# Clustered attention in float32: probability tiles of 512 columns, codes by DMA, value sums off VectorE, a table load moved, due times replaced

## The chip, the core and the metric

The kernel runs on one core of one Trainium2 chip. The core has TensorE (PE in the profile), VectorE (DVE), ScalarE (ACT) and GpSimd (POOL); SyncE (SP) only issues DMAs here. Each engine takes its own instructions strictly in the order of the program. The metric is the device time of one execution in microseconds: 778.55 us before the change, the median of 3 runs that lie between 778.21 and 780.17.

## The reference

Sixteen heads (2 batches of 8), each of 768 tokens and width 64. Queries and keys attend to each other only when their nearest centroid is the same one; two matrix products with relu6 follow.

```
q_assign = argmax(q_n @ c_n^T)           # 16 centroids a head, normalized
k_assign = argmax(k_n @ c_n^T)
scores   = where(q_assign == k_assign, q @ k^T / 8, -1e9)
attn     = exp(scores - max); attn /= sum(attn) + 1e-9
x = attn @ v                             # -> 1536 x 512
h = (x @ w1) * (x @ w2); x = h @ w3 @ w_out
y = x @ w_in; y = y * clip(y + 3, 0, 6) / 6; out = y @ w_out2
```

All weights arrive as float64 and are converted on the chip with integer operations. Products are made in three float32r passes: every operand is split into a high part (ScalarE rounds it to float32r) and a low part (the rest, a subtraction).

## The kernel before

**The order is planned.** Every operation is entered with an engine (or several to choose from), a cost, what it needs, buffers ("rings") that it takes and drops, and a due time. The method `order` walks through them: among the operations that could start first on each engine it picks the one with the smallest due time. The table `SHIFT` adds a correction to single due times. What comes out is one list, and each engine runs its part of it in that order. So a change of costs, of an operation's engine or of `SHIFT` moves instructions on all engines.

**Attention, one head after the other.** `prep_ops(h)` loads q, k and v, splits them, transposes them on PE (`stack_T`, tile `pt`), copies them out (`stack_C`) and duplicates a half by DMA (`stack_D`). `assign_mm` computes the centroid products (tile `pa`), and nine small steps (`oh_step`, `oh0` to `oh8`) make the one-hot codes of the assignments; the last is a DVE transpose into the tile `cd`. `codes_C` then copies four pieces of 16 x 384 from `cd` into the operands `kA` and `qA`, which makes the mask a part of the score product. It runs on ACT or DVE (entry `Co`), whichever the plan finds free first.

`attn_ops(h)` has six chunks of 128 queries. For each, PE computes scores (`S1` of 512 columns and `S` of 256, two matmuls each, tile `pst`), DVE takes the maximum over 768 columns (`mx`, tile `den`), ACT the exponential with its row sum (`ex`, tile `p`; six buffers). The probabilities are then transposed on PE: `p_T` puts three 128 x 128 blocks into a PSUM bank (tile `ptr`, one of three buffers of ring `s`), 12 such tiles a head; `p_hi` rounds the 384 columns to `ph` on ACT, `p_lo` writes the rest to `pl` on DVE, and `av` multiplies by the values, with `vs` holding the high and low part of v in its two halves. So the product `av` has two halves of 64 rows that must be added. ACT copies one half to tile `O` (`o_copy`, `oc`). For the first two pairs of heads ACT copies the other half too (`o_copy2`, `oa`) and POOL adds them (`o_sum`, `os`); for the other six pairs DVE adds the halves (`o_add`), reading one of them from PSUM. `oap(h)` decides which. The row sums get 1e-9 added and are inverted on DVE (`den_recip`, `dr`), go through PE and DRAM (`rd`, `rdb`), and POOL multiplies them in (`pair_mul`, `pm`).

**Beside attention** PE has work that fills gaps: first the product of w3 and w_out (tiles `pt` for its transposes, `psw`), whose operands come from the conversions `c0` to `c5` (ACT, POOL, and three DVE steps), then, from head 9 on, the products of the first batch (`ab_mm`, tile `psab`). At the start `idle` matmuls keep PE busy. After attention come `psx`, a second `psab`, `psh` and `po`, the two feed-forward stages.

**SP** holds all DMA issues in one queue, also in the plan's order; an issue that waits for its buffer holds all behind it.

At the very start ACT loads a function table for its copies, one for the square root of the centroids' norms (`cen_2`) and one for the exponential (`warm_exp`).

The places by line: `warm_exp` 286, `cen_2` 309, `codes_C` 415, `p_T` 549, `p_hi` 555, `p_lo` 561, `av` 565, `oap` 585, `o_sum` 594, `o_add` 597, `den_recip` 603. The copies and subtractions themselves are recorded at their helpers' lines: 205 and 214 on POOL, 208 on DVE, 211 on ACT.

Of the kernel before, what the change touches and what calls it, by code (L numbers as in the profile page):

```python
# [160 lines left out]
def cluster_attention_moe_kernel(  # L161
# [387 lines left out]
    def p_T(h, hf, s, i):  # L549
        pt = ptr[i] = ps_s.tile([128, 512], F32, tag="s", name="ptr")  # L550
        for c in range(3):
            nc.tensor.transpose(pt[:, blk(c)], pps[h, 3 * hf + c][:, blk(2 * s + i)], id_f)  # L552
# [1041 lines left out]
```

## Time and profile before

| | us |
|---|---|
| median of 3 runs | 778.55 |
| the profiled execution | 778.79 |
| its span, first to last instruction | 777.0 |
| PE busy | 754.0 (97%) |
| DVE busy | 662.7 (85%) |
| ACT busy | 542.0 (70%) |
| POOL busy | 266.3 (34%) |

The granted TensorE clock is 0.998 of full over the span, so the clock is not a matter here. A matmul's row lasts until its modelled end and overlaps the next, so "busy" says less of PE than the interval from one start to the next does. The first instruction of the stage behind attention (`psx`) starts at 395.31 us; up to there the span is called the attention stage below.

### The profile page before, as it was taken

How to read it: one execution, taken by the hardware profiler on the slowest of the kernel's cores; microseconds unless marked ns; L12 is line 12 of the kernel's file. 1: busy time of each engine (PE TensorE's matmuls, PEld its weight loads, DVE VectorE, ACT ScalarE, POOL GpSimd, SP SyncE). 2: the span in 40 equal slices, each digit the busy share in tenths (PEclk: the TensorE clock that was granted, in tenths of full speed). 3: DMA queues.
4: the chain of work that ended last, by engine and by line, in shares of the span. 5: the costliest groups of instructions: out<-in, count | busy, mean ns of one | idle time of the engine just before them, and what ended most of it. 6: DMA issues, size and time to landing. Idle time of an engine off the chain costs nothing.

```text
span 777.0 us, 12420 instructions
## 1 busy us (share of the span) xinstructions
PE 754.0 (97%) x4266; PEld 682.0 (88%) x4266; DVE 662.7 (85%) x1184; ACT 542.0 (70%) x1070; POOL 266.3 (34%) x295
## 2 busy tenths in 40 slices
PE   6899999999999999999999999999999999999998
PEld 5678787888888899999899999999989889898986
DVE  6989999999999989899998899979999877767742
ACT  6779898887887787777763665757666667555544
POOL 4835656454563564443233111621222211010100
PEclk9999999999999999999999999999999999999999
DMA  7453343323343543334234543374544424212102
GB/s 227 125 173 107 106 133 105 108 87 116 116 116 89 160 140 112 112 113 135 91 136 136 164 148 123 106 247 149 174 152 123 139 91 150 82 55 67 41 14 81
DMA packets 57038, 94.20 MB, mean 121 GB/s; under 512 B 5168, under 2 KB 33936, under 8 KB 56976
## 3 DMA queue, kind: packets, MB, share of 16 engines
q1 hardware_dynamic: 56976, 93.43, 38.3%
q8 instruction: 33, 0.54, 0.3%
q14 instruction: 29, 0.24, 0.1%
HBM read 71.34 MB, written 15.78 MB: 112 GB/s over the span
## 4 chain that ended last, share of the span: by engine, by line
PE 57%; DVE 10%; ACT 5%; POOL 2%; issue 2%; DMA 1%; SPq 0%; DVEq 0%; ACTq 0%
PE po L1486 14%; PE psh L1442 13%; PE psab L1131 8%; PE psab L880 6%; PE psx L994 4%; PE pst L527 4%; PE av L572 3%; PE ptr L552 3%; POOL cvt L744 2%; DMA m_gb<-set 1%; DVE pl L208 1%; ACT p L544 1%; DVE den L536 1%; DVE cvs L753 1%; DVE m_whl L208 1%
## 5 line engine op out<-in xcount | busy, mean ns | idle before, releaser
L744 POOL TENSOR_SCALAR cvt<-cvt 128x512 f32<-128x512 f32 x72 | 73.5, 1023 | 172.5 <-ACT cvt L211 147.0
L211 ACT ACTIVATE ph<-ptr 128x384 fp32r<-128x384 f32 x192 | 90.7, 487 | 37.5 <-PE ptr L552 36.8
L208 DVE TENSOR_TENSOR pl<-ptr,ph 128x384 fp32r<-128x384 f32 x192 | 102.9, 549 | 11.6 <-ACT ph L211 9.9
L544 ACT ACTIVATE p<-pst,den 128x768 f32<-128x768 f32 x96 | 86.5, 901 | 11.7 <-DVE den L536 11.3
L536 DVE TENSOR_REDUCE den<-pst 128x1 f32<-128x768 f32 x96 | 90.8, 946 | 4.5 <-PE pst L527 3.6
L552 PE MATMUL ptr<-id_f,p 128*128 128x128 f32 x576 | 88.1, 274 | 2.0 <-DVE rdr L614 0.5
L880 PE MATMUL psab<-xT,abhl 128*128 128x384 f32 x384 | 86.6, 348 | 0.1
L552 PEld LDWEIGHTS ptr<-id_f,p 128*128 128x128 f32 x576 | 68.9, 140 | 11.8 <-DVE pl L208 2.6
L527 PE MATMUL pst<-kB,qB 128*128 128x512 f32 x192 | 71.1, 374 | 3.5 <-ACT p L544 2.8
L572 PE MATMUL av<-ph,vs 128*128 128x384 f32 x192 | 69.4, 362 | 0.1
L880 PEld LDWEIGHTS psab<-xT,abhl 128*128 128x128 f32 x384 | 64.5, 189 | 2.1 <-DVE g L890 0.7
L572 PE MATMUL av<-pl,vs 128*128 128x384 f32 x192 | 65.0, 339 | 0.5 <-DVE pl L208 0.4
L527 PE MATMUL pst<-kA,qA 128*128 128x512 f32 x192 | 64.2, 339 | 0.0
L753 DVE SCALAR_TENSOR_TENSOR cvs<-raw,cvs 128x512 int32<-128x512 int32 x72 | 54.6, 761 | 0.4
L211 ACT ACTIVATE cvt<-raw 128x512 f32<-128x512 f32 x72 | 47.9, 669 | 8.3 <-DMA raw<-in_moe_w_dram 4.2
L211 ACT ACTIVATE m_sn<-psh 128x384 f32<-128x384 f32 x64 | 31.0, 485 | 32.4 <-PE psh L1442 32.0
L804 PE MATMUL psw<-woh,wT 128*128 128x512 f32 x128 | 51.9, 416 | 0.7 <-ACT W L211 0.4
L1464 ACT ACTIVATE tt<-m_sn,three 128x384 f32<-128x384 f32 x48 | 29.5, 616 | 32.8 <-DVE m_sn L1452 25.2
L757 DVE SCALAR_TENSOR_TENSOR cvs<-cvt,cvs 128x512 int32<-128x512 int32 x72 | 50.2, 702 | 0.2
L527 PEld LDWEIGHTS pst<-kB,qB 128*128 128x128 f32 x192 | 36.1, 188 | 12.9 <-ACT p L544 9.8
L1486 PE MATMUL po<-m_hl,m_gv 128*128 128x512 f32 x171 | 46.2, 394 | 0.0
L749 DVE TENSOR_SCALAR cvs<-cvt 128x512 int32<-128x512 int32 x72 | 33.9, 478 | 7.4 <-POOL cvt L744 5.1
(206 smaller groups left out, 1934.6 us busy)
## 6 DMA issues: line engine op xcount, KB each, us to landing
raw<-in_moe_w_dram SPq DMA_DIRECT2D x32, 512.0 KB, 3.6
m_gb<-set SPq DMA_DIRECT2D x64, 256.0 KB, 3.4
raw<-in_moe_w_out_dram SPq DMA_DIRECT2D x24, 512.0 KB, 3.3
raw<-in_moe_w_in_dram SPq DMA_DIRECT2D x16, 512.0 KB, 4.2
set<-cvs SPq DMA_DIRECT2D x32, 256.0 KB, 4.2
abp<-cvs SPq DMA_DIRECT2D x16, 256.0 KB, 2.0
b_gv<-abp SPq DMA_DIRECT2D x16, 256.0 KB, 3.0
qn<-in_q_dram SPq DMA_DIRECT2D x16, 192.0 KB, 4.9
```

The lines of the kernel that those rows point to most:

```text
L208: nc.vector.tensor_tensor(out=out, in0=a, in1=b, op=ALU.subtract)
L211: nc.scalar.activation(out=out, in_=in_, func=AF.Copy, **kw)
L527: x = mm(out=psr[:, t, ks_], lhsT=TT["q" + nm, h][:, i, cs_], rhs=flat(TT["k" + nm, h])[:, ks_], start=st, stop=sp)
L536: done["mx", n] = [other_banks(nc.vector.tensor_reduce(out=dens[h][:, 0, c:c + 1], in_=psS[h, c], axis=AX.X, op=ALU.max, negate=True), ("S ...
L544: done["ex", n] = [other_banks(nc.scalar.activation(out=flat(p), in_=psS.pop((h, c)), func=AF.Exp, bias=d[:, 0, c:c + 1], accum_out=d[:, 1 ...
L552: nc.tensor.transpose(pt[:, blk(c)], pps[h, 3 * hf + c][:, blk(2 * s + i)], id_f)
L572: mm(out=t[:, 0:HF], lhsT=vs_t[h][:, 2 * s + i, :], rhs=x_[:, i, :], start=(s == 0 and i == 0 and n == 0), stop=(s == 2 and i == 1 and n = ...
L744: (nc.gpsimd.tensor_scalar if e == "pool" else ts)(out=tf, in0=tf, scalar1=H_MAX, scalar2=-H_MAX, op0=ALU.min, op1=ALU.max)
L753: stt(out=s, in0=raws.pop(key)[:, :, 0], scalar=29, in1=s, op0=ALU.logical_shift_right, op1=ALU.bitwise_or)
L880: mm(out=ps[:, 0:HF], lhsT=s[:, w, a, blk(kk)], rhs=xT0[0][:, x_, kk, hf * HF:hf * HF + HF], start=(kk == 0 and n == 0), stop=(kk == KD - ...
L1442: mm(out=ps[:, 0:HF], lhsT=left(p, l, a, kk), rhs=x[:, x_, kk, :], start=(st and kk == 0 and m == 0), stop=(kk == 1 and m == 2), skip_grou ...
L1486: mm(out=outs[b, c], lhsT=g[:, a, blk(c % 3)], rhs=w[:, w_, :], start=(first and a == 0 and w_ == 0), stop=(last and a == 1))
```

## The change

Five edits and a new table:

1. The transposed probabilities are cut anew: the 36 blocks of a head are taken in the order in which `av` reads them and put four to a PSUM bank, so a head has nine tiles of 512 columns and not twelve of 384. `ph` and `pl` are one tile each, of three 512-column places used in turn. The fifth tile holds two blocks of the first half of the queries and two of the second.
2. From head 1 on the four code pieces go by DMA from SP's queue (due a little earlier: 2.3 units ahead of the head where it was 1.8); head 0 keeps the copies.
3. `oap` holds for seven of the eight pairs: ACT copies both value halves and POOL adds them; the last pair keeps DVE's addition.
4. The addition of 1e-9 becomes an ACT operation of its own (`dd`), and DVE only inverts.
5. A square root of a constant, due before all else on ACT, loads the root's table first.
6. `SHIFT` is another table.

```
-    "warm": 1.7, ("Tq", 0, 1): 1.6, ("Dq", 0): 1.6, ("Tk", 0, 0): 10.3, ("oh1", 0): -4.4, ("ex", 0, 1): -0.1,
+    "cen2": 10.2, ("idle", 4): 0.1, ("idle", 5): -0.1, ("cT", 0): 1.9, ("lk", 0): 0.5, ("CkB", 0, 0): -0.1,
...
-        "p": NP, "ph": 2, "pl": 2, "den": 2, ...
+        "p": NP, "ph": 3, "den": 2, ...
...
+    op("root", "act", 0.2, lambda: warm(AF.Sqrt), due=-60)
+    op("warm", "act", 1.4, lambda: warm(AF.Exp), ["cen2"], due=-13.85)
...
     def codes_C(e, h, nm, hf):
-        copy_on(e, t[0:NCL, hf, :], codes[h][r0:r0 + NCL, :])
+        if h:
+            nc.sync.dma_start(out=t[0:NCL, hf, :].bitcast(F32), in_=codes[h][r0:r0 + NCL, :])
+        else:
+            copy_on(e, t[0:NCL, hf, :], codes[h][r0:r0 + NCL, :])
...
+            dd = b - (2.3 if h else 1.8) + 0.5 * hf
...
+                    op(("C" + nm, h, hf), "dma", 0.2, lambda nm=nm, hf=hf: codes_C(None, h, nm, hf), nd, due=due, lat=2.0, **kw)
...
+    def p_blocks(n):
+        return [(f // 18, f % 18 // 3, f % 3) for f in range(4 * n, 4 * n + 4)]
+    def p_cols(n):
+        return slice(512 * (n % 3), 512 * (n % 3) + 512)
+    def p_T(h, n):
+        pt = phl[h, n] = ps_s.tile([128, 512], F32, tag="s", name="ptr")
+        for j, (hf, kb, c) in enumerate(p_blocks(n)):
+            nc.tensor.transpose(pt[:, blk(j)], pps[h, 3 * hf + c][:, blk(kb)], id_f)
+    def p_hi(h, n):
+        copy_act(PHL[0][:, p_cols(n)], phl[h, n])
+    def p_lo(h, n):
+        sub_dve(PHL[1][:, p_cols(n)], phl.pop((h, n)), PHL[0][:, p_cols(n)])
...
     def oap(h):
-        return h // 2 < 2
+        return h // 2 < 7
...
+    def den_add(h):
+        nc.scalar.activation(out=d[:, 2, :], in_=d[:, 1, :], func=AF.Copy, bias=1e-9)
     def den_recip(h):
-        nc.vector.tensor_scalar(out=d[:, 2, :], in0=d[:, 1, :], scalar1=1e-9, scalar2=None, op0=ALU.add)
         nc.vector.reciprocal(out=d[:, 2, :], in_=d[:, 2, :])
...
+        for n in range(9):
+            u = b + LT + 2 * n / 3
+            op(("pT", h, n), "pe", 0.436, ..., due=u, take=("s",), drop=("p",) * 3 if n in (4, 8) else ())
+            op(("ph", h, n), "act", 0.48, ..., due=u + 0.1, take=("ph",), ...)
+            op(("pl", h, n), "dve", 0.6, ..., due=u + 0.2, drop=("s",))
```

What the change does to the order shows at three places. First ACT from its first instruction on, before (`qA` and `kA` are cleared rows, `cst` is the centroids' norm, `qs` and `ks` the split q and k of head 0, `warm` the dummy exponential):

```order
L211 ACT_TABLE_LOAD
L211 ACTIVATE qA<-three 64x768
L211 ACTIVATE kA<-three 64x768
L310 ACT_TABLE_LOAD
L310 ACTIVATE cst<-cst 128x1
L211 ACTIVATE qs<-qn 128x6x64
L288 ACT_TABLE_LOAD
L288 ACTIVATE warm<-three 128x1
L211 ACTIVATE ks<-kn 128x6x64
```

and now:

```order
L303 ACT_TABLE_LOAD
L303 ACTIVATE warm<-three 128x1
L225 ACTIVATE qA<-three 64x768
L225 ACTIVATE kA<-three 64x768
L225 ACTIVATE qs<-qn 128x6x64
L326 ACTIVATE cst<-cst 128x1
L303 ACT_TABLE_LOAD
L303 ACTIVATE warm<-three 128x1
L225 ACTIVATE ks<-kn 128x6x64
```

Of three table loads two are left, and the one ahead of the norm is gone; the split of q now stands ahead of the norm.

Second, the codes of head 8. Before, they stand on ACT between probability tiles (`ph`) and an exponential (`p,den`):

```order
L211 ACTIVATE ph<-ptr 128x384
L211 ACTIVATE kA<-cd 16x384
L211 ACTIVATE qA<-cd 16x384
L211 ACTIVATE ph<-ptr 128x384
L211 ACTIVATE kA<-cd 16x384
L544 ACTIVATE p,den<-pst,den 128x768
L211 ACTIVATE qA<-cd 16x384
L211 ACTIVATE ph<-ptr 128x384
```

Now they are four issues in SP's queue, behind the load of a weight (`raw`), the broadcast of a row sum (`rdb`) and the store of a converted weight (`abp`), and ahead of the load of v:

```order
L755 DMA raw<-in_moe_w_dram 128x4x256
L650 DMA rdb<-rd_116 64x768
L899 DMA abp_85<-cvs 128x512
L434 DMA kA<-cd 16x384
L434 DMA qA<-cd 16x384
L434 DMA kA<-cd 16x384
L434 DMA qA<-cd 16x384
L383 DMA vn<-in_v_dram 128x384
```

All four have left ACT. On SP they can be held by what stands ahead of them.

Third, DVE around the same code transpose (`cd`), before (`cvs` are conversions of a weight, `den` the maxima and row sums):

```order
L453 STREAM_TRANSPOSE cd<-ohs 128x384
L601 TENSOR_TENSOR T<-av,O 64x384
L536 TENSOR_REDUCE den<-pst 128x1
L208 TENSOR_TENSOR pl<-ptr,ph 128x384 x2
L753 SCALAR_TENSOR_TENSOR cvs<-raw,cvs 128x512
L813 TENSOR_TENSOR W_493<-W_493,psw 128x512
L536 TENSOR_REDUCE den<-pst 128x1
L208 TENSOR_TENSOR pl<-ptr,ph 128x384 x2
L757 SCALAR_TENSOR_TENSOR cvs<-cvt,cvs 128x512
L605 TENSOR_SCALAR den<-den 128x6
L606 RECIPROCAL den<-den 128x6
```

and now:

```order
L472 STREAM_TRANSPOSE cd<-ohs 128x384
L222 TENSOR_TENSOR pl<-ptr,ph 128x512
L779 TENSOR_SCALAR cvs<-cvt 128x512
L558 TENSOR_REDUCE den<-pst 128x1
L222 TENSOR_TENSOR pl<-ptr,ph 128x512
L787 SCALAR_TENSOR_TENSOR cvs<-cvt,cvs 128x512
L783 SCALAR_TENSOR_TENSOR cvs<-raw,cvs 128x512
L558 TENSOR_REDUCE den<-pst 128x1
L222 TENSOR_TENSOR pl<-ptr,ph 128x512
L843 TENSOR_TENSOR W_496<-W_496,psw 128x512
L787 SCALAR_TENSOR_TENSOR cvs<-cvt,cvs 128x512
```

Between two maxima there were two subtractions of 384 columns; now there are one or two of 512. The addition of value halves (`T<-av,O`) and the small addition ahead of the reciprocal are gone.

## Rows read from the trace of the kernel before

**Rows 1.** Stretches: length, busy us (instructions) of PE, PEld, DVE, ACT, POOL; clock, DMA
```profile
0.00:22.00 22.00, 15.96 (x66) 12.67 (x67) 15.64 (x37) 14.07 (x24) 11.62 (x37) 0.92 0.76 245
22.00:75.00 53.00, 49.16 (x287) 40.42 (x286) 48.45 (x88) 43.21 (x92) 29.16 (x38) 1.00 0.44 129
75.00:275.00 200.00, 193.26 (x1207) 168.28 (x1205) 186.73 (x349) 167.66 (x362) 105.58 (x123) 1.00 0.38 113
275.00:375.00 100.00, 99.76 (x640) 94.41 (x640) 91.50 (x169) 75.89 (x166) 43.36 (x51) 1.00 0.38 121
375.00:395.30 20.30, 19.50 (x112) 17.22 (x110) 18.46 (x30) 14.30 (x25) 5.43 (x4) 1.00 0.48 154
395.30:640.00 244.70, 243.16 (x1305) 230.11 (x1306) 219.44 (x376) 151.47 (x268) 59.72 (x37) 1.00 0.44 141
```

**Rows 2.** Timeline of PE within head 8: start us, us, instruction
```profile
205.82 0.39 PE L804 MATMUL psw<-woh,wT 128*128 128x512 f32 x1
206.05 0.40 PE L804 MATMUL psw<-wol,wT 128*128 128x512 f32 x1
...
206.52 0.28 PE L527 MATMUL pst<-kB,qB 128*128 128x256 f32 x1
206.63 0.29 PE L527 MATMUL pst<-kA,qA 128*128 128x256 f32 x1
206.76 0.82 PE L552 MATMUL ptr<-id_f,p 128*128 128x128 f32 x6
207.33 0.42 PE L572 MATMUL av<-ph,vs 128*128 128x384 f32 x1
207.59 0.34 PE L572 MATMUL av<-pl,vs 128*128 128x384 f32 x1
```

**Rows 3.** The chain in order of time: start us, us, what
```profile
395.31 32.35 PE psx L994 x185
```

**Rows 4.** Groups by shape: busy us, mean ns of one, idle us before and releaser
```profile
L208 DVE TENSOR_TENSOR pl<-ptr,ph 128x384 fp32r<-128x384 f32 x192 | 102.9, 549 | 11.6 <-ACT ph L211 9.9
L211 ACT ACTIVATE ph<-ptr 128x384 fp32r<-128x384 f32 x192 | 90.7, 487 | 37.5 <-PE ptr L552 36.8
L208 DVE TENSOR_TENSOR wT<-pt,wT 128x512 fp32r<-128x512 f32 x16 | 10.8, 675 | 0.8 <-ACT wT L211 0.7
L211 ACT ACTIVATE wT<-pt 128x512 fp32r<-128x512 f32 x16 | 9.5, 596 | 5.2 <-PE pt L776 5.2
L211 ACT ACTIVATE kA<-cd 16x384 fp32r<-16x384 f32 x29 | 15.2, 523 | 3.1 <-DVE cd L453 2.5
L601 DVE TENSOR_TENSOR T<-av,O 64x384 f32<-64x384 f32 x24 | 13.2, 550 | 1.9 <-ACT O L211 1.4
L211 ACT ACTIVATE T<-av 64x384 f32<-64x384 f32 x8 | 3.9, 484 | 0.1
L595 POOL TENSOR_TENSOR T<-T,O 128x768 f32<-128x768 f32 x2 | 3.7, 1843 | 1.9 <-ACT T L211 1.9
L605 DVE TENSOR_SCALAR den<-den 128x6 f32<-128x6 f32 x16 | 7.7, 483 | 2.2 <-ACT p L544 2.2
```

**Rows 5.** Timeline of ACT at the start: start us, us, instruction
```profile
3.62 1.28 ACT L310 ACT_TABLE_LOAD   x1
4.91 0.20 ACT L310 ACTIVATE cst<-cst 128x1 f32<-128x1 f32 x1
```

**Rows 6.** SP's copies within SBUF (line 411): issue ns min/median/max; time to landing
```profile
L411 SPq DMA_DIRECT2D kA<-kB x16: 461/467/539, 11.5 to 336.8; - x16
...
DMA to landing us min/median/max: 2.5/2.6/4.2
```

**Rows 7.** Timeline: one conversion step of DVE alone, and one beside a subtraction of POOL
```profile
23.62 1.27 POOL L205 TENSOR_TENSOR wol<-cvs,woh 128x512 fp32r<-128x512 f32 x1
...
23.80 1.38 DVE L749 TENSOR_SCALAR cvs<-cvt 128x512 int32<-128x512 int32 x1
...
50.97 0.37 DVE L749 TENSOR_SCALAR cvs<-cvt 128x512 int32<-128x512 int32 x1
```

More of the change, by code (lines that the diff above doesn't have):

```diff
@@ L284, in cluster_attention_moe_kernel, with warm @@
     op("id", "dve", 0.14, lambda: nc.vector.tensor_copy(id_r, id_f), due=-40)
-    def warm_exp():
-        W_["warm"] = at.tile([128, 1], F32, tag="warm", name="warm")
-        nc.scalar.activation(out=W_["warm"], in_=three, func=AF.Exp)
+    def warm(func):
+        if "warm" not in W_:
+            W_["warm"] = at.tile([128, 1], F32, tag="warm", name="warm")
+        nc.scalar.activation(out=W_["warm"], in_=three, func=func)
     def zero_rows(t):
         copy_act(t[0:64], three[0:64].unsqueeze(2).to_broadcast([64, 2, HF]), scale=0.0)
-    op("warm", "act", 1.4, warm_exp, ["cen2"], due=-13.85)
+    op("root", "act", 0.2, lambda: warm(AF.Sqrt), due=-60)
+    op("warm", "act", 1.4, lambda: warm(AF.Exp), ["cen2"], due=-13.85)
     for i, t in enumerate((qA_[1], kA_[1])):
@@ L487, in prep_ops @@
         for hf in range(2):
-            dd = b - 1.8 + 0.5 * hf
-            fop("Co", ("Ck", h, hf), {"a": 0.375, "d": 0.47}, lambda e, hf=hf: codes_C(e, h, "k", hf),
-                (("oh8", h), ("Dk", h)), due=dd + 0.05)
-            fop("Co", ("Cq", h, hf), {"a": 0.375, "d": 0.47}, lambda e, hf=hf: codes_C(e, h, "q", hf),
-                (("oh8", h), ("Dq", h)), due=dd + 0.06, after=[("Ck", h, 0), ("Ck", h, 1), ("Cq", h, 0)] if hf else (),
-                drop=("cd",) if hf else ())
+            dd = b - (2.3 if h else 1.8) + 0.5 * hf
+            for nm in "kq":
+                last = nm == "q" and hf
+                kw = dict(after=[("Ck", h, 0), ("Ck", h, 1), ("Cq", h, 0)] if last else (), drop=("cd",) if last else ())
+                nd, due = (("oh8", h), ("D" + nm, h)), dd + (0.06 if nm == "q" else 0.05)
+                if h:
+                    op(("C" + nm, h, hf), "dma", 0.2, lambda nm=nm, hf=hf: codes_C(None, h, nm, hf), nd, due=due, lat=2.0, **kw)
+                else:
+                    fop("Co", ("C" + nm, h, hf), {"a": 0.375, "d": 0.47}, lambda e, nm=nm, hf=hf: codes_C(e, h, nm, hf), nd, due=due, **kw)
         op(("pa", h), "pe", 0.7, lambda: assign_mm(h), [("CqB", h, 0), ("CqB", h, 1), ("CkB", h, 0), ("CkB", h, 1),
@@ L547, in sexp @@
         pps[h, c] = flat(p)
[L549 to L552, printed above, removed]
-        phl[h, hf, s, i, "t"] = pt
-    def p_hi(h, hf, s, i):
-        if i == 0:
-            phl[h, hf, s] = (at.tile([128, 2, HF], F32R, tag="ph", name="ph", bufs=2),
-                             at.tile([128, 2, HF], F32R, tag="pl", name="pl", bufs=2))
-        copy_act(phl[h, hf, s][0][:, i], phl[h, hf, s, i, "t"][:, 0:HF])
-    def p_lo(h, hf, s, i):
-        ph, pl = phl[h, hf, s]
-        sub_dve(pl[:, i], phl.pop((h, hf, s, i, "t"))[:, 0:HF], ph[:, i])
+    PHL = []
+    def p_blocks(n):
[7 more added lines that the diff above has]
+    def p_hi(h, n):
+        if not PHL:
+            PHL.extend(at.tile([128, 1536], F32R, tag=t, name=t) for t in ("ph", "pl"))
+        copy_act(PHL[0][:, p_cols(n)], phl[h, n])
+    def p_lo(h, n):
+        sub_dve(PHL[1][:, p_cols(n)], phl.pop((h, n)), PHL[0][:, p_cols(n)])
     def av(h, hf, s):
@@ L568, in av @@
         t = avs[h, hf]
-        ph, pl = phl.pop((h, hf, s))
         for i in range(2):
-            for n, x_ in enumerate((ph, pl)):
-                mm(out=t[:, 0:HF], lhsT=vs_t[h][:, 2 * s + i, :], rhs=x_[:, i, :],
+            c0 = HF * ((2 * s + i + 2 * hf) % 4)
+            for n, x_ in enumerate(PHL):
+                mm(out=t[:, 0:HF], lhsT=vs_t[h][:, 2 * s + i, :], rhs=x_[:, c0:c0 + HF],
                    start=(s == 0 and i == 0 and n == 0), stop=(s == 2 and i == 1 and n == 1))
@@ L657, in attn_ops @@
                 drop=("r",))
+        for n in range(9):
+            u = b + LT + 2 * n / 3
+            op(("pT", h, n), "pe", 0.436, lambda n=n: p_T(h, n), sorted({("ex", h, 3 * x[0] + x[2]) for x in p_blocks(n)}),
+               due=u, take=("s",), drop=("p",) * 3 if n in (4, 8) else ())
+            op(("ph", h, n), "act", 0.48, lambda n=n: p_hi(h, n), (("pT", h, n),), due=u + 0.1, take=("ph",),
+               after=[("ph",) + divmod(9 * h + n - 1, 9)] * (h + n > 0))
+            op(("pl", h, n), "dve", 0.6, lambda n=n: p_lo(h, n), (("ph", h, n),), due=u + 0.2, drop=("s",))
         for hf in range(2):
@@ L660, in attn_ops @@
                 u = b + 3 * hf + s + LT
[L661 to L669 removed]
+                m = 3 * hf + s
                 op(("av", h, hf, s), "pe", 0.65, lambda hf=hf, s=s: av(h, hf, s),
[L671 removed]
+                   [("pl", h, n) for n in {(3 * m) // 2, (3 * m + 2) // 2}] + [("vlo", h)] + [("av", h, hf, s - 1)] * (s > 0),
                        due=u + LA,
[L673 removed]
+                   take=("a",) if s == 0 else (), drop=("ph",) * (1 + m % 2) + (("vs",) if hf and s == 2 else ()))
             if oap(h):
@@ L686, in attn_ops @@
         e = b + NC
-        op(("dr", h), "dve", 0.35, lambda: den_recip(h), [("ex", h, c) for c in range(NC)], due=e + 1)
+        op(("dd", h), "act", 0.2, lambda: den_add(h), [("ex", h, c) for c in range(NC)], due=e + 0.9)
+        op(("dr", h), "dve", 0.2, lambda: den_recip(h), (("dd", h),), due=e + 1)
         op(("dT", h), "pe", 0.11, lambda: den_T(h), (("dr", h),), due=e + 1.2, take=("s",), drop=("den",),
```

14 lines of the change are left out of this document (2 added, 12 removed), and 52 rows, old and new, of the table SHIFT.

## The prediction

> **What bounds the kernel now.** I read the stretches first [rows 1]. PE is the busiest engine in every one, and behind 395.3 us there is nothing to win on it: 243.2 of 244.7 us busy. The reader should see the pair PE and DVE next: from 75 to 275 us PE has 193.3 of 200 us and DVE 186.7 (93%), while from 275 to 375 PE has 99.8 of 100 with DVE at 91.5. Since a busy PE row runs on to its modelled end, I took what PE's work is worth from the starts of neighbours in the timeline [rows 2]: a 512-column matmul 0.23 us (205.82 to 206.05), one of 256 columns 0.115 (206.52 to 206.63), one of 384 columns 0.175 (185 `psx` in 32.35 us [rows 3]), and six transposes with one 384-column matmul 0.83 (206.76 to 207.59), so 0.109 a transpose.
>
> The attention stage ends at 395.31 us, where `psx` starts [rows 3]. By the code's loops it holds 192 score pairs of both widths (192 x 0.345 = 66.2), 848 transposes (576 of probabilities, 192 of q and k, 64 of w3, 16 of row sums: 92.4), 832 matmuls of 384 columns (384 values, 64 centroids, 384 `psab`: 145.6) and 232 of 512 (192 `psw`, 40 idle ones: 53.4). That is 357.6 us, so 37.7 us are lost to waits. They spread, at the mean of 0.156 us an instruction over the counts of the stretches [rows 1], as about 11.7 us before 22 us, 8.3 up to 75, 12.0 up to 275, 0.3 up to 375 and 2.9 up to 395. The prize is the middle, some 20 us, where DVE feeds PE: a maximum for every chunk, a low part for every tile, and three conversion steps for the weights of the filling work. Behind 275 us PE fills its gaps with `psab`, whose operands come sooner, and loses next to nothing.
>
> **The change part by part.** PE: nothing is removed. The 36 transposes a head stay 36, and a group of transposes shows no price of its own in [rows 2], so nine groups for twelve are worth 0.
>
> DVE in the attention stage [rows 4]. Low parts: 192 x 0.549 = 105.4 become 144 of 512 columns, which is the shape of w3's low part at 0.675, 97.2: -8.2. Value sums: 20 of 24 go at 0.550: -11.0. The addition of 1e-9: 16 x 0.483: -7.7. Of the 64 code copies eight stand on DVE, one is left, priced as on ACT at 0.523: -3.7. The new plan gives DVE four more copies of transposed q and k (384 columns, as the low parts 0.549): +2.2. Sum -28.4 us, 1.8 a head.
>
> ACT: high parts 192 x 0.487 = 93.5 become 144 x 0.596 = 85.8: -7.7. Code copies 56 to 3 at 0.523: -27.7. Value halves +20 x 0.484 = +9.7 [rows 4]. The addition is not in the trace on ACT; between a one-column operation at 0.20 [rows 5] and the 384 columns of 0.487 [rows 4] I take 0.20, which has nearly its size: +3.2 (to 7.8). The four copies to DVE: -1.9. Sum about -24 us.
>
> POOL: five more sums at 1.84 [rows 4], +9.2 on an engine that is busy 53% of the middle.
>
> The table: a load of 1.28 us stands right ahead of the norm on ACT [rows 5] and goes; the split of q, 384 columns or some 0.49 us, now stands there in its place. Everything to the first score hangs on this chain: -0.8, bounds -1.3 and 0 (0 if k's arrival decides).
>
> The codes: on ACT the three pieces that the first scores need take 3 x 0.523 = 1.6 us at least. By DMA three issues of 0.467 and a landing of 2.6 make 4.0 us, up to 5.6 with the slowest landing of 4.2 [rows 6], so 2.4 to 4.0 later. What hides it is the plan: in DVE's order the transpose that ends the codes stands two or more maxima ahead of its head's first one for 12 of 15 heads. From 22 to 395 us there are 16 heads, 23.3 us each and 3.9 a chunk, so that is over 7 us. Heads 1, 2 and 10 have one maximum, 3.9 us: 0.1 to 1.7 each may show. Below nothing there is nothing, since the score cannot start sooner than before by this. I take +1.0 for all, bounds 0 and +5. In SP's queue a load of v and the next weight stand behind the codes; v is wanted a head's third later, and SP's four issues take 1.9 us.
>
> [...]
>
> The fifth tile, half of one half and half of the other, waits for the fifth exponential where the sixth old tile waited for the third, and gives back the first three `p` buffers later by about half a chunk, 1.9 us. By the due times they are wanted half a chunk after that; 0, and up to 1.9 a head if that cover is gone.
>
> The sum: the stretch from 75 to 275 is 200 of the 373 us, so 15.2 of DVE's 28.4 fall into it. PE can take at most the 12.0 it loses there; nothing would come if its waits were round trips alone. In 192.5 us the rest of DVE's work, 171.5, would be 89% of the stretch, under the 91.5% at which PE loses next to nothing [rows 1]; but the fill hangs on conversions there, which stay. So I take 7.5 of 12.0. From 22 to 75 us, 3.0 of 8.3, since much of that is the first heads' own chain. Start -0.8, codes +1.0, the stage behind attention 0 with bounds of 2 either way (its order moves a little, and DVE is at 90% there). Together -10.3. Against the profiled execution's 778.8 us (span 777.0) this is 768.5; the median of the runs shown is 0.2 lower, so 768.3.
>
> **The rivals.** *The relief does not reach PE* (0.15). The idle rows point at partners: low parts wait 9.9 us for ACT's high parts and those 36.8 for PE [rows 4], a ring of short round trips that a lighter DVE does not shorten, and the longer tiles even stretch by 0.1 each. Against it: 93% is close to full. Then the start and 2 us of the middle remain: 776.
>
> *POOL holds ACT* (0.10, the slower side). `T` and `O` have one buffer each. Now ACT, not DVE, writes `T`; its first copy of the next pair waits until POOL has summed, multiplied and split the last one. Three POOL steps at the sum's 1.84 and a rounding are 6.5 us. In ACT's order the copy stands three exponentials, some 11.6 us, behind the last copy of the old pair, so it decides once POOL is more than 5 us late, and POOL's queue is one engine that waits for conversions. All exponentials stand behind the waiting copy and PE's scores behind those. At 3 us for six pairs, 18 less 10: 786.
>
> *POOL's sums hold DVE* (0.14). A conversion step took 0.37 alone and 1.38 beside a POOL subtraction that ended at 24.89, just before it did at 25.18 [rows 7]. If each of the five new sums held DVE for its whole 1.84 us, 9.2 of the 28.4 would be gone, and with it a third of the gain: 772. The Trainium skill, "SBUF — State Buffer", section "SBUF: two separate sides", has it as a rule: the port pair that the two share is locked for a whole instruction, not divided. Rows 7 agree with it. I leave it a rival and not a term, since rows 7 show it for the conversion steps alone, of which few stand beside any one sum.
>
> *All of the middle's loss goes* (0.11): PE without waits from 22 us on, as from 275 to 375. 20.3 + 0.8 less: 757.5.
>
> **How the numbers follow.** The forecast has 0.50, with its own range 762 to 773. A run of this kernel can tell 0.3%, 2.3 us, from no change. Faster by more: 0.50 + 0.14 + 0.11 and half of the first rival, 0.07, are 0.82; within: its other half, 0.08; slower: 0.10. The range of 757 to 779 leaves out half of the best case and the slower one, some 0.15.
>
> **What would show it.** Right: DVE's busy time before the first `psx` down by 25 to 32 us and ACT's by 20 to 28, `psx` starting at 383 to 387, and the stretch behind it as long as before. `pl` rows at 0.67 and `ph` rows at 0.60, the norm's root near 4.1 us. The codes: rows of the first score of a head released by DMA, under 1 us in sum. Wrong: PE idle behind a DMA of the codes at most heads, `T` rows of ACT waiting for POOL, or `psx` earlier but the final stage longer by as much, because the conversions for it had not moved ahead.

## The result, and the profile after

The changed kernel takes 773.26 us (median of five executions, 770.61 to 773.97) against 778.55 for the kernel before on the same chip: ratio 0.992, 95% interval 0.9897 to 0.9944. A second set of executions gave 772.31 us, ratio 0.9916 (0.9899 to 0.9933). It is faster by 0.8%, as forecast in sign, and within the range of 757 to 779 us; the forecast of 768.3 us was 4 to 5 us too low, and of its own range, 762 to 773 us, the first median lies just outside and the second just inside. The gain in medians is 5.3 and 6.9 us where 10.3 was forecast. The execution shown below is the fastest of the five, 770.61 us with a span of 768.8.

The stretches of the changed kernel, with the columns of [rows 1] (length; busy us and instructions of PE, PEld, DVE, ACT, POOL; clock; DMA share; GB/s):

```profile
0.00:22.00 22.00, 15.55 (x69) 12.54 (x70) 15.56 (x37) 14.25 (x26) 12.95 (x37) 0.92 0.78 248
22.00:75.00 53.00, 49.07 (x293) 40.73 (x292) 47.74 (x83) 39.62 (x82) 32.06 (x40) 1.00 0.47 139
75.00:275.00 200.00, 196.99 (x1275) 179.30 (x1274) 184.72 (x314) 164.88 (x340) 121.48 (x135) 1.00 0.43 127
275.00:375.00 100.00, 99.66 (x640) 94.97 (x639) 84.64 (x141) 73.44 (x146) 43.33 (x45) 1.00 0.36 113
375.00:382.70 7.70, 6.01 (x32) 5.11 (x30) 5.35 (x10) 3.07 (x6) 1.84 (x1) 1.00 0.70 217
382.70:507.50 124.80, 124.77 (x719) 124.58 (x720) 110.11 (x193) 71.58 (x124) 35.19 (x14) 1.00 0.44 141
507.50:640.00 132.50, 128.62 (x635) 115.64 (x634) 117.08 (x200) 87.55 (x158) 22.39 (x20) 0.99 0.43 137
```

and the row of the chain of waits at which the attention stage ends (start us, us, what):

```profile
382.73 33.38 PE psx L1024 x191
```

This row is not quite the one of [rows 3], which starts 12.6 us later: it holds 191 of the first 192 `psx` matmuls, and that one 185. All 192 by themselves, before and after (duration in ns min/median/max, then the first and the last start in us):

```profile
L994 PE MATMUL psx<-gh,Whl x192: 333/335/447, 393.3 to 427.3; 128*128 128x384 f32 x192
L1024 PE MATMUL psx<-gh,Whl x192: 334/334/446, 381.7 to 415.8; 128*128 128x384 f32 x192
```

So 395.31 us is the start of the eighth `psx`, not of the first, and six matmuls, 1.0 us, have to come off the difference. Two readings matter. First, the same `psx` comes 11.5 us earlier than before (415.8 against 427.3). The gain is in the middle: from 75 to 275 us PE now issues 1275 matmuls where it issued 1207 [rows 1], and 68 at the prediction's 0.156 us are 10.6 us. Second, what follows has become longer: from the last of these `psx` to the end it is 777.0 - 427.3 = 349.7 us before and 768.8 - 415.8 = 353.0 now. So 11.5 us were won and 3.3 given back, and the net is the 8.2 us by which the spans differ.

The groups that answer to [rows 4] (busy us, mean ns of one, idle us before and releaser):

```profile
L222 DVE TENSOR_TENSOR pl<-ptr,ph 128x512 fp32r<-128x512 f32 x144 | 97.8, 681 | 12.2 <-ACT ph L225 11.3
L225 ACT ACTIVATE ph<-ptr 128x512 fp32r<-128x512 f32 x144 | 84.9, 595 | 31.6 <-PE ptr L582 28.3 <-PE av L599 0.9 <-PE pst L549 0.6
L549 PE MATMUL pst<-kA,qA 128*128 128x512 f32 x96 | 37.9, 395 | 0.7 <-DMA kA<-cd 0.7
L225 ACT ACTIVATE T<-av 64x384 f32<-64x384 f32 x28 | 13.6, 484 | 0.5
L632 ACT ACTIVATE den<-den 128x6 f32<-128x6 f32 x16 | 3.4, 211 | 0.0
```

The new shapes cost what was taken for them from the trace before: 0.681 for a low part (0.675 taken), 0.595 for a high part (0.596), 0.211 for the addition on ACT (0.20, the end of the range that it was read from). The scores wait for a DMA of the codes once, 0.7 us in all (1.0 taken), and ACT's `T` copies wait 0.5 us in all, so POOL does not hold them.

Where the 3.3 us went is seen first at the start of the second feed-forward stage. PE's rows there (start us, us, instruction, in brackets the idle time before it and what ended it):

```profile
510.65 1.33 PE L1472 MATMUL psh<-m_x1b,m_gB 128*128 128x384 f32 x6 [0.76 <-ACT m_sn L225]
513.96 1.33 PE L1472 MATMUL psh<-m_x1b,m_gB 128*128 128x384 f32 x6 [1.98 <-DVE m_sn L1482]
```

and what VectorE does ahead of the addition that PE waits for (the last row):

```profile
504.58 1.56 DVE L1379 TENSOR_TENSOR m_gb<-m_gb 128x256 f32<-128x256 f32 x4 [2.29 <-DMA m_gb<-set]
506.81 1.49 DVE L222 TENSOR_TENSOR m_gB<-m_gb,m_gB 128x1280 fp32r<-128x1280 f32 x1 [0.67 <-ACT m_gB L225]
508.22 0.68 DVE L222 TENSOR_TENSOR m_w<-m_gb,m_w 128x512 fp32r<-128x512 f32 x1
509.41 0.82 DVE L779 TENSOR_SCALAR cvs<-cvt 128x512 int32<-128x512 int32 x1 [0.51 <-POOL cvt L774]
510.26 1.64 DVE L783 SCALAR_TENSOR_TENSOR cvs<-raw,cvs 128x512 int32<-128x512 int32 x1
511.83 0.41 DVE L779 TENSOR_SCALAR cvs<-cvt 128x512 int32<-128x512 int32 x1
512.17 0.68 DVE L787 SCALAR_TENSOR_TENSOR cvs<-cvt,cvs 128x512 int32<-128x512 int32 x1
512.77 0.68 DVE L783 SCALAR_TENSOR_TENSOR cvs<-raw,cvs 128x512 int32<-128x512 int32 x1
513.37 0.54 DVE L1482 TENSOR_TENSOR m_sn<-m_sn,psh 128x384 f32<-128x384 f32 x1
```

Five conversion steps of two weight planes (lines 779 to 787) stand between the split `m_w` and the addition. In the kernel before the same two follow one another:

```profile
521.03 0.68 DVE L208 TENSOR_TENSOR m_w<-m_gb,m_w 128x512 fp32r<-128x512 f32 x1
522.05 0.56 DVE L1452 TENSOR_TENSOR m_sn<-m_sn,psh 128x384 f32<-128x384 f32 x1 [0.33 <-ACT m_sn L211]
```

From the same `psx` to the split it is 93.7 us before (427.3 to 521.03) and 92.4 after (415.8 to 508.22), so VectorE reaches the split no later than it did; from there to the addition it is 1.0 and 5.2 us. The row of 1.64 us has a reason of its own: it stands beside a subtraction of POOL from 509.92 to 511.36, and the same step alone takes 0.68 (at 512.77). That is the lock of [rows 7] on another step. The Trainium skill, "SBUF — State Buffer", section "SBUF: two separate sides", has the port pair locked for a whole instruction; the trace agrees, with 1.0 us lost beside one of 1.44.

A third thing follows the pause. PE's clock in steps of 2 us (columns as above):

```profile
513.60:515.60 2.00, 1.64 (x8) 1.60 (x9) 1.32 (x4) 1.41 (x3) 0.00 (x0) 0.88 0.97 358
515.60:517.60 2.00, 2.00 (x8) 2.00 (x7) 1.89 (x4) 0.83 (x3) 0.00 (x0) 0.50 0.47 153
517.60:519.60 2.00, 2.00 (x10) 2.00 (x10) 1.20 (x3) 1.33 (x3) 0.00 (x0) 0.77 0.80 185
```

The granted clock falls to 0.50, the 1.2 GHz level, after PE had stood idle for 0.76 and then for 1.98 us, and is back at 1.00 at about 519 us. PE issued 26 matmuls in these 6 us, of which the first 0.36 belong to the pause. Behind the first `psx` PE's waits add up to 3.9 us, where they were 1.5 before: the two above and 1.1 us for `m_gv`, a low part of VectorE's, ahead of `po` at 525.70 (0.5 before).

### The profile page after: what moved, and what is told of

Read it like the earlier page. It is cut to its first block, busy times and chain, and to the rows that moved or that the text cites. A ratio compares the mean times of both kernels' runs of the same rounds, so it can differ in the third digit from the quotient of the medians.

```text
span 768.8 us, 12438 instructions
## 1 busy us (share of the span) xinstructions
PE 745.8 (97%) x4266; PEld 684.4 (89%) x4266; DVE 640.8 (83%) x1100; ACT 523.3 (68%) x1001; POOL 280.7 (37%) x297
## 4 chain that ended last, share of the span: by engine, by line
PE 83%; DVE 8%; issue 3%; ACT 2%; DMA 2%; POOL 1%; SPq 0%; ACTq 0%; DVEq 0%; POOLq 0%
PE po L1516 17%; PE psh L1472 15%; PE pst L549 8%; PE psab L910 8%; PE av L599 8%; PE psab L1161 7%; PE ptr L582 7%; PE psw L834 5%; PE psx L1024 4%; PE pa L442 1%; DVE cvs L783 1%; DMA m_gb<-set 1%; PE idle L332 1%; PE pt L806 1%; DVE cvs L787 1%
## 5 line engine op out<-in xcount | busy, mean ns | idle before, releaser
L774 POOL TENSOR_SCALAR cvt<-cvt 128x512 f32<-128x512 f32 x72 | 78.2, 1088 | 199.5 <-ACT cvt L225 169.1
L222 DVE TENSOR_TENSOR pl<-ptr,ph 128x512 fp32r<-128x512 f32 x144 | 97.8, 681 | 12.2 <-ACT ph L225 11.3
L225 ACT ACTIVATE ph<-ptr 128x512 fp32r<-128x512 f32 x144 | 84.9, 595 | 31.6 <-PE ptr L582 28.3
L558 DVE TENSOR_REDUCE den<-pst 128x1 f32<-128x768 f32 x96 | 91.2, 950 | 15.6 <-PE pst L549 14.5
L582 PE MATMUL ptr<-id_f,p 128*128 128x128 f32 x576 | 84.7, 272 | 0.0
L910 PE MATMUL psab<-xT,abhl 128*128 128x384 f32 x384 | 83.2, 345 | 0.4 <-DVE g L920 0.4
L787 DVE SCALAR_TENSOR_TENSOR cvs<-cvt,cvs 128x512 int32<-128x512 int32 x72 | 52.7, 739 | 0.3
L1516 PE MATMUL po<-m_hl,m_gv 128*128 128x512 f32 x144 | 39.3, 394 | 1.1 <-DVE m_gv L222 1.1
```

The source lines that it names most:

```text
L222: nc.vector.tensor_tensor(out=out, in0=a, in1=b, op=ALU.subtract)
L225: nc.scalar.activation(out=out, in_=in_, func=AF.Copy, **kw)
L558: done["mx", n] = [other_banks(nc.vector.tensor_reduce(out=dens[h][:, 0, c:c + 1], in_=psS[h, c], axis=AX.X, op=ALU.max, negate=True), ("S ...
L582: nc.tensor.transpose(pt[:, blk(j)], pps[h, 3 * hf + c][:, blk(kb)], id_f)
L774: (nc.gpsimd.tensor_scalar if e == "pool" else ts)(out=tf, in0=tf, scalar1=H_MAX, scalar2=-H_MAX, op0=ALU.min, op1=ALU.max)
L910: mm(out=ps[:, 0:HF], lhsT=s[:, w, a, blk(kk)], rhs=xT0[0][:, x_, kk, hf * HF:hf * HF + HF], start=(kk == 0 and n == 0), stop=(kk == KD - ...
```

## The experiments

All are forms of the changed kernel except one. "`psx` starts" is the second of the 192 matmuls; for the two forms of the kernel before, whose row of the chain starts later, the eighth's start less six matmuls. "behind" is the span less the start of the last of the 192. Both come from one profiled execution each, the medians from four to six. Each ratio is to the kernel before on the same chip.

| kernel | `psx` starts, us | behind, us | median, us | ratio to before |
|---|---|---|---|---|
| before | 394.28 | 349.7 | 778.55 to 779.25 | 1 |
| changed | 382.73 | 353.0 | 773.26 | 0.9920 (0.9897 to 0.9944) |
| a0: changed, again | 384.39 | 352.2 | 772.31 | 0.9916 (0.9899 to 0.9933) |
| e1: two planes' steps on DVE behind the addition | 382.76 | 353.5 | 773.85 | 0.9927 (0.9908 to 0.9945) |
| e1c: all their steps behind it | 384.49 | 350.6 | 771.23 | 0.9897 (0.9879 to 0.9915) |
| e10: eight conversion steps left out | 385.45 | 350.4 | 770.46 | 0.9886 (0.9867 to 0.9905) |
| e6: root's table where it was | 384.06 | 355.0 | 773.54 | 0.9930 (0.9911 to 0.9949) |
| e4: sums on DVE, order kept | 388.56 | 351.6 | 775.02 | 0.9949 (0.9929 to 0.9969) |
| e3: codes on ACT, order kept | 403.37 | 352.8 | 790.38 | 1.0145 (1.0127 to 1.0164) |
| e2: old table | 399.22 | 354.6 | 788.66 | 1.0111 (1.0091 to 1.0131) |
| e8: no table | 394.71 | 355.0 | 784.26 | 1.0059 (1.0040 to 1.0079) |
| e9: the kernel before, no table | 402.21 | 350.0 | 787.46 | 1.0110 (1.0090 to 1.0130) |
| e3n: no table, codes planned on ACT and DVE | 399.90 | 354.2 | 788.49 | 1.0122 (1.0104 to 1.0140) |
| e4n: no table, sums planned on DVE | 403.01 | 351.9 | 790.16 | 1.0160 (1.0132 to 1.0188) |

**a0, the changed kernel again.**

> The changed kernel once more, as the one that the other runs are compared with. Both theories of the give-back expect the same: a median of 771 to 774 us, psx from 382 to 384 us (before: 395.31), and a pause of TensorE of about 3 us at the start of the second feed-forward stage (510 to 515 us of the span), in which it waits for VectorE's addition m_sn<-m_sn,psh. If the pause came from one unlucky execution, it is absent here or below 1 us.

The pauses are there again, 1.05 and 2.00 us, so they belong to the order. The clock did not fall:

```profile
515.30:517.30 2.00, 1.40 (x8) 1.38 (x9) 1.32 (x4) 1.17 (x3) 0.00 (x0) 1.00 0.93 333
517.30:519.30 2.00, 2.00 (x13) 1.89 (x12) 2.00 (x5) 1.22 (x3) 0.00 (x0) 1.00 0.49 178
```

In the two windows that start just before the end of the second pause, the first execution issued 16 matmuls (513.6 to 517.6) and this one 21; five at 0.175 us are 0.9 us. With the 2.4 us by which PE's waits grew, that makes up the 3.3 us of the first execution; in this one, with 4.4 us of waits and the clock at full, 2.5 us were given back. `psx` came at 384.39 us, just past the 384 that was expected.

a0, e1, e1c and e10 have the order of the changed kernel up to `psx`; with the first execution their starts of `psx` go from 382.73 to 385.45, mean 383.96. That spread, 2.7 us, is the measure for a `psx` read from one execution, and 10.3 us (394.28 less the mean) is the better figure for what the attention stage gained; the kernel before has only one execution in it.

**e1, the addition first.**

```
 op(("c3",) + key, "dve", ..., take=("cvs",), lock=True,
+   after=[("ca", 0, 1)] * (key in (("set", 9, 1), ("set", 10, 0))))
```

> The changed kernel, but the five conversion steps of the weight planes that stand ahead of the addition m_sn<-m_sn,psh at the start of the second feed-forward stage may come only behind it. Theory 'order' (the pause is there because VectorE is given these conversions first): the pause of 3.1 us (0.76 + 1.98 and what follows on ACT) goes, and with it the lower granted clock behind it (about 2 us); the time is 4 to 6 us below the changed kernel's, 767 to 769 us. Rival 'backlog' (VectorE's conversions are late by then and only come somewhere else): the wait comes back at a later psh or po of the same stage, and the time is 0 to 1 us below. psx at 382 to 384 us in either.

The time did not change, and the theory did not get the 4 to 6 us it had claimed. The wait for the addition went, the one ahead of it grew (1.05 us in a0), and a new one came much later (PE, columns as above):

```profile
511.40 2.38 PE L1473 MATMUL psh<-m_x1b,m_gB 128*128 128x384 f32 x12 [1.49 <-ACT m_sn L225]
...
588.45 0.96 PE L1473 MATMUL psh<-m_x,m_gB 128*128 128x384 f32 x4 [2.18 <-DVE tt L1499]
```

The first is ScalarE's, whose two copies `cvt<-raw` of the same planes still stood ahead of `m_sn` in its row:

```profile
508.31 1.24 ACT L225 ACTIVATE cvt<-raw 128x512 f32<-128x512 f32 x2
509.44 0.49 ACT L225 ACTIVATE x2f<-psx 128x384 f32<-128x384 f32 x1
509.81 1.16 ACT L225 ACTIVATE m_whl<-m_gb 128x512 fp32r<-128x512 f32 x2
510.85 0.50 ACT L225 ACTIVATE m_sn<-psh 128x384 f32<-128x384 f32 x1
```

That left two readings, order on both engines or too much work for VectorE whatever the order, and the next two runs were made for them.

**e1c, both planes behind the addition from their first step.** The same `after=` stands at `c0`, the step on ScalarE.

> The changed kernel with the conversions of the same two planes behind the addition m_sn<-m_sn,psh from their first step on, ScalarE's (cvt<-raw) included; in the first form only VectorE's and what follows were moved, and ScalarE's two, 1.24 us, still stood ahead of its m_sn<-psh, for which PE then waited 1.65 us. Theory 'order': of the 5.6 us that PE loses between 500 and 550 us under the changed kernel 1 to 2 stay (before: 0.9), the granted clock stays full there, no wait takes their place, and the time is 4 us lower, 767 to 769.5 us. Rival 'backlog' (VectorE has more to do up to 620 us than the stage leaves it, whatever the order): PE loses 2 to 5 us at later psh or po between 520 and 620 us instead, and the time stays at 771 to 774 us.

**e10, less work on VectorE, order kept.**

```
 def c_low():
     s = cvo[key]
+    if key in LEFT:   # planes (9,1), (10,0), (10,1), (11,0)
+        raws.pop(key); return
     ...               # and the same in c_sign
```

> The changed kernel in its own order, without VectorE's last two conversion steps (8 instructions, 5.5 to 6.5 us) of four weight planes at the start of the second feed-forward stage: their values are wrong, and nothing else is left out. Theory 'backlog': the pause before the addition m_sn<-m_sn,psh (2.15 us) and the one before po (1.3 us) go, with the lower clock behind the first, no later wait comes, and the time is 3.5 to 5 us lower, 767.5 to 769.5 us. If the second feed-forward stage still loses 4 us or more, what PE waits for there is not VectorE's load but the landing of the fetch m_gb<-set behind which VectorE and ScalarE stand (VectorE waited 2.3 us for it, ScalarE 5.8 us).

Both helped in part, and neither as much as its theory claimed: 771.23 us where 767 to 769.5 was expected of e1c, which is the lower end of its rival's 771 to 774, and 770.46 where 767.5 to 769.5 was expected of e10. In e1c the stretch behind `psx` fell from 352.2 and 353.0 to 350.6 us, the clock stayed at 1.00, and two waits of PE are left early in the stage:

```profile
516.21 1.32 PE L1473 MATMUL psh<-m_w,m_gB 128*128 128x384 f32 x6 [1.12 <-ACT m_sn L225]
522.05 1.19 PE L1517 MATMUL po<-m_hl,m_whl 128*128 128x512 f32 x4 [0.84 <-DVE m_whl L222]
```

e10 came to 350.4 us, with a wait of 1.62 us for ACT's `m_sn` and 0.93 for DVE's `m_gv`. Both have some 2.8 us of PE's waits in all behind the first `psx`, where the changed kernel has 3.9 and 4.4 and the kernel before 1.5. So the order of the conversions is one cause, worth some 2 of the 2.5 to 3.3 us in single executions; but with the order kept, eight instructions less gave as much, so the amount of VectorE's work ahead of the addition serves as well, and the two runs do not set the one against the other. The two were not tried together. The 0.7 to 0.9 us that are left are less than executions of one kernel differ by. VectorE's wait for the next planes, 2.26 us in e1c, is there in both:

```profile
506.76 1.56 DVE L1380 TENSOR_TENSOR m_gb<-m_gb 128x256 f32<-128x256 f32 x4 [2.26 <-DMA m_gb<-set]
```

It is not what sets the new kernels apart: the kernel before had such a wait too, 1.32 us, and there VectorE's first `m_gb` step started 2.1 us ahead of the last `psx` of the stage (516.92 and 519.0), in the changed kernel 2.9 us ahead of it (504.58 and 507.5). An earlier fetch was not tried. e1c is the best version with all of the computation; its interval reaches into that of the changed kernel, so it beats the kernel before for certain and the changed one by some 1 to 2 us that a set of this size hardly separates.

**e2, the old table with the new operations.**

> The changed kernel with the table of due times of the kernel before, so the edits of operations without the new search. Theory 'operations' (what was gained in the attention stage comes from the relief of VectorE and ScalarE, whatever the table): psx at 384 to 387 us, and the time at 771 to 777 us, within 4 us of the changed kernel. Rival 'table' (the gain is the new order): psx at 390 to 396 us and 778 us or more.

The rival won, and by more than it claimed: `psx` at 399.22 us, 4.9 behind that of the kernel before. The table fits only in part: 14 of its 97 entries name probability tiles that the new operations do not have, and act on nothing. The stretch ahead of the middle and the middle, to be read against [rows 1] and against the changed kernel's rows above:

```profile
22.00:75.00 53.00, 46.40 (x251) 37.48 (x250) 43.62 (x68) 32.66 (x66) 27.53 (x35) 0.94 0.42 124
75.00:275.00 200.00, 192.73 (x1212) 169.37 (x1213) 181.79 (x307) 159.25 (x327) 110.99 (x129) 1.00 0.40 119
```

The delay against the kernel before arises ahead of 75 us: PE issues 251 matmuls from 22 to 75 us where it issued 287, 5.6 us at 0.156, with the granted clock at 0.94 for 1.00. In the middle VectorE is busy for 181.8 of 200 us, 4.9 less than before, and PE issues 1212 matmuls, five more than before. VectorE has room there, and PE hardly gets it. The group of low parts shows what the room turns into (before: 9.9 us for `ph`; changed kernel: 11.3):

```profile
L208 DVE TENSOR_TENSOR pl<-ptr,ph 128x512 fp32r<-128x512 f32 x144 | 98.0, 682 | 20.8 <-ACT ph L211 20.3
```

**e8 and e9, both kernels without a table.**

```
-SHIFT = { ... }
+SHIFT = {}
```

> The changed kernel with an empty table of shifted due times, so its operations in the order that the planner's rules give by themselves. To be compared with the kernel before under the same empty table. Theory 'operations' (VectorE's and ScalarE's relief is worth some 10 us whatever the table): psx 8 to 14 us before that of the other one. Rival 'order' (after the run with the old table, 17 us later at psx, the likelier now: the relief is worth little until the order is fitted to it): psx within 4 us of the other one's, or behind it, and both far above their tuned forms, 790 us or more.

> The kernel before with an empty table of shifted due times. Theory 'operations': 795 to 805 us, psx 8 to 14 us behind that of the changed kernel without a table. Rival 'order': psx within 4 us of that one's.

The rows of the middle, first e8 and then e9:

```profile
75.00:275.00 200.00, 190.94 (x1195) 169.19 (x1194) 177.34 (x303) 156.03 (x319) 113.39 (x131) 0.99 0.40 119
75.00:275.00 200.00, 186.20 (x1148) 160.89 (x1147) 186.79 (x340) 160.83 (x343) 105.29 (x121) 0.99 0.36 107
```

On the same count of matmuls `psx` stands at 394.71 against 402.21 us: 7.5 us apart, just under the band of "operations", 8 to 14 us, and outside the 4 us of "order". The difference is in the middle, 47 matmuls or 7.3 us at 0.156, with VectorE 9.5 us less busy. An account of the 11.5 us is then: 7.5 for the operations when neither order is fitted, and 4.0 more because the new search gains more on the new operations (12.0, from 394.71 to 382.73) than the old one did on the old (7.9, from 402.21 to 394.28). How firm the 7.5 is, is a matter for e4n below. The old table on the new operations is worse than none, by 4.5 us. The totals are 3.2 us apart, and both lower than expected: 784.26 us where the rival had 790 or more, 787.46 where "operations" had 795 to 805.

The column "behind" says one thing more. The kernels with the new operations whose order behind `psx` was left alone have 351.6 to 355.0 us there, with the new table, the old one or none, and both forms of the kernel before have 350. The first have the pair of pauses at the second feed-forward stage, the last two one of 0.65 and 0.48 us. The give-back comes with the new operations and not with the search; the table names no operation behind the attention stage.

**e3 and e3n, the codes without the DMA.**

```
-        if h:
-            nc.sync.dma_start(out=t[0:NCL, hf, :].bitcast(F32), in_=codes[h][r0:r0 + NCL, :])
+        if h:
+            copy_act(t[0:NCL, hf, :], codes[h][r0:r0 + NCL, :])
```

> The changed kernel, with the 20 row codes of heads 1 to 15 copied by ScalarE in the place where the changed kernel issues a DMA; the order stays. My costing (a DMA that lands in time costs about 1 us in all, and ScalarE has the room for the copies): psx within 1.5 us of the changed kernel's and the time within 0.3% of it. Rival 'ScalarE is late at these places' (each copy of some 0.37 us moves the evictions behind it): psx 3 to 5 us later, 775 to 778 us.

> The changed kernel without a table, and with the 60 copies of the row codes of heads 1 to 15 planned on ScalarE or VectorE again as in the kernel before (in place of the DMAs), so that the planner makes room for them. If the codes' DMAs are what is worth 18 us (as the run with the copies put on ScalarE in the places of the DMAs would have it), psx is 15 us or more behind that of the changed kernel without a table. If that loss came from copies in places that were not planned for them, psx is within 5 us of it; 28 us of work on two engines that are 92% and 82% busy in the middle of the attention stage can still be worth some 3 us.

The edit moves 60 pieces, four for each of 15 heads, where the expectation speaks of 20 row codes. With the order kept, `psx` starts 19.4 us later than the mean of its five: 31 more microseconds on ScalarE, two thirds of which reach PE. My costing was wrong by an order of magnitude here, and the rival by four times. The rows show how a step can cost more than itself (ACT, columns as above):

```profile
214.19 0.52 ACT L225 ACTIVATE kA<-cd 16x384 fp32r<-16x384 f32 x1
214.73 0.52 ACT L225 ACTIVATE qA<-cd 16x384 fp32r<-16x384 f32 x1
215.26 0.48 ACT L225 ACTIVATE O<-av 64x384 f32<-64x384 f32 x1
215.76 0.52 ACT L225 ACTIVATE kA<-cd 16x384 fp32r<-16x384 f32 x1
216.29 0.52 ACT L225 ACTIVATE qA<-cd 16x384 fp32r<-16x384 f32 x1
216.72 0.57 ACT L225 ACTIVATE ph<-ptr 128x512 fp32r<-128x512 f32 x1
```

A DMA's place in the plan is where it may be issued; four copies in that place are, with one of `O` between them, a block of 2.5 us ahead of the eviction `ph`, on which the low part, the values and the next transposes wait. VectorE then stands 14.8 us in the middle stage waiting for `ph`, where it was 5.1 in the changed kernel. When the planner makes room for them (e3n), the loss is 5.2 us, just past the 5 of the second reading. So, without a table, the DMA of the codes is worth some 5 us, not the 18 us.

**e4 and e4n, the sums back on VectorE.**

```
-copy_act(Ts[h // 2][rows, hf, :], avs.pop((h, hf))[rows, 0:HF])
+tt(out=Ts[h // 2][rows, hf, :], in0=avs.pop((h, hf))[rows, 0:HF], in1=W_["o"][rows, hf], op=ALU.add)  # heads 4 to 13
```

> The changed kernel with the value halves of heads 4 to 13 summed by VectorE again (20 sums of some 0.55 us) in the place of ScalarE's copy, and without GpSimd's sum; the order stays. My costing (VectorE has 11 us less room, of which the prediction gave PE about a third): psx 2 to 5 us later, 775 to 778 us. Rival 'a fixed order gives most of an added instruction to PE' (the copies of the codes gave 0.34 us each): psx 7 us or more later, 780 us.

> The changed kernel without a table, and with the sums of the value halves of heads 4 to 13 planned on VectorE from the output bank again as in the kernel before. psx stood at 394.7 us without a table, 403.3 us in the kernel before without a table, and 399.9 us with the codes copied by the engines. If the parts add up, the sums, the wider tiles and the constant share the 3.4 us that the codes leave: psx 1 to 3 us later, 395.7 to 397.7 us. Rival 'the planner's own order moves by several us at any edit': psx before 394.7 us, or behind 399 us.

ScalarE's copies and GpSimd's sums for these heads go with the edit. With the order kept, 20 sums of 0.551 us move `psx` by 4.6 us (388.56 against 383.96): inside the band, 0.42 us for each microsecond on VectorE. The row of the middle has VectorE at 188.61 us and PE at 1253 matmuls, 22 fewer than in the changed kernel. Without a table the same edit moves `psx` by 8.3 us, outside the band: the rival, that the planner's own order moves by several us at any edit, is what came. Its middle:

```profile
75.00:275.00 200.00, 186.34 (x1148) 163.35 (x1146) 178.47 (x304) 144.03 (x296) 107.97 (x125) 0.98 0.41 122
```

VectorE is busy for 1.1 us more than in e8, and PE has lost all 47 matmuls that e8 had over e9, a part of them to the granted clock (0.98 for 0.99). Codes and sums together would then be 13.5 us, more than the 7.5 of the whole change: without a fitted order the parts do not add up, and what each is worth there is left open. The 7.5 us come from two such orders too, one of each kind, so they carry the same luck, several us of it.

**e6, the root's table where it was.**

```
 def warm(func):
+    if func == AF.Sqrt:
+        return
```

> The changed kernel without the first Sqrt, so that ScalarE loads the root's table where the centres' norms need it, as before. The forecast's value for this edit: PE's lag behind its own work at 22 us of the span 0.8 us larger, and as much at the end (bounds 0 to 1.3 us), 773 to 774 us. Rival 'hidden' (TensorE's start waits for another load): no difference above 0.2 us in the first 22 us.

`psx` at 384.06 us lies in the spread of the five, so the edit has no effect that these runs can tell; the 0.8 us are not shown. The norm's root does start later, at 5.44 us where it was 4.10, but at 22 us PE has issued 65 matmuls, as in a0, with 69 in the first execution. The median, 773.54 us, is what the forecast's value for the edit asked for, and by itself tells nothing. This run and e8 have the longest stretch behind `psx`, 355.0 us, and its rows show why: the same two pauses (1.74 and 2.00 us), and the lower clock for three windows, in which PE issues 17 matmuls in 6 us, the rest of the second pause included:

```profile
515.00:517.00 2.00, 0.72 (x2) 0.72 (x3) 1.32 (x4) 0.74 (x2) 0.00 (x0) 0.50 0.80 254
517.00:519.00 2.00, 2.00 (x7) 2.00 (x7) 2.00 (x5) 1.17 (x3) 0.00 (x0) 0.50 0.77 269
519.00:521.00 2.00, 2.00 (x8) 2.00 (x8) 0.81 (x2) 0.57 (x2) 0.00 (x0) 0.50 0.56 156
```

## Why the prediction was right, and where it was not

- **End of the attention stage, 383 to 387 us: right, by terms that were off both ways.** 382.73, and 383.96 as the mean of five; on the same count of matmuls 11.5 and 10.3 us were gained, and 10.3 was the sum. The middle gave 10.6 us where 7.5 were taken; from 22 to 75 us it gave about 1 (293 matmuls for 287, six at 0.156) where 3.0 were taken; the start gave nothing that e6 can show where 0.8 was taken, though the norm's root came at 4.10 us as forecast; the codes' DMAs cost 0.7 us of waiting where 1.0 was taken. That these add up so well is luck.
- **Relief of the engines: right in the main, a little small.** By the stretches VectorE's busy time up to `psx` fell from 360.8 to 338.0 us, 22.8, where 25 to 32 was forecast, and ScalarE's from 315.1 to 295.3, 19.8, where 20 to 28 was. The stretches count overlapping instructions once; summed over the groups up to `psx` it is 25.0 (398.1 to 373.1) and 26.2 (356.9 to 330.7). Two terms of VectorE were off: the low parts' rows fell from 102.9 to 97.8 us, 5.1 where 8.2 was taken, and the 135 conversion steps, which the sum left alone, rose from 89.1 to 91.2.
- **The reason for the gain: half right.** The prediction read VectorE's 93% as what bounds PE and shared out its relief. e8 against e9 bears that out in the middle. e2 and e4n refute it as a rule: with VectorE 4.9 us less busy than before an unfitted order gave PE five matmuls, and with VectorE as free as in e8 another gave it 47 fewer. In the changed kernel VectorE did not even fall to the 89% that was worked out; it is busy for 92% of the middle (184.7 of 200 us), beside 68 more matmuls. "The relief does not reach PE" was given 0.15; with the old table that is nearly what came in the middle. The gain needs both, and the prediction had no term for the new search, 4.0 us of the 11.5 by the account above.
- **POOL holds ACT, and POOL's sums hold DVE: not seen.** The `T` rows of ACT waited 0.5 us in all, and the low parts kept their 0.68 us; the 2.1 us by which the conversion steps rose are all that these rows leave for such a hold. The lock itself showed up elsewhere, in the pause at 510 us.
- **The stage behind attention, 0 with bounds of 2: the step that failed.** It gave back 3.3 us in the profiled execution and 2.5 in a0. "Its order moves a little" was the whole of its working; the orders of both kernels, which could be read, showed the conversions ahead of the addition. The sign named in the text, `psx` earlier and the final stage longer, is what came, but not for the cause named there: 45 of the 72 planes were converted by the start of `psx` in both kernels. What differs is which steps stand ahead of one addition, and how much work they are. The stretch looked longer by 1.0 us than it was, since the start that the prediction took for `psx` was that of the eighth one before and of the second one after.
- **The sum.** -11.5 and +3.3 against -10.3 and 0, in the execution shown. The median lies 2.7 us above it; the three longer executions of that set, spans of 771.5 us and more, had a mean granted clock of 0.991 to 0.993, the two shorter ones 0.995 and 0.997. The clock's fall at that pause, there in the first execution and in e6 and absent in a0, is one thing that differs between executions of one order.

## What to carry to other kernels

When an order is written out and fitted, ask of an edit not how busy its engine is but what stands next in the row behind it: here the same 0.5 us copy cost two thirds of itself in a place made for a DMA, and a quarter of that where, without a table, room was planned. Compare operations with the order taken out of both sides (both tables emptied) before crediting either, and allow for luck even then: without a table one small edit moved `psx` by 8.3 us. And follow a shorter stage to the next one's first instructions: an earlier start there is worth what stands ahead of them.
